# A 12-head attention and two MLPs on one core: the weights' product w3·w_out decoded by another sequence, its maxima taken from copies, its last row groups and column halves in turn

## The chip, the core and the metric

One core of a Trainium2 chip runs the whole program. The metric is device time in microseconds (us) of that core, the median of several runs. Engines: PE is TensorE, DVE is VectorE, ACT is ScalarE, POOL is GpSimd, SP issues most of the transfers.

## The reference

```python
attn = softmax(scale * einsum('bhij,hg->bgij', q @ k.T, w_pre))   # 4 batches, 12 heads, 448 positions
x = einsum('bhij,hg->bgij', attn, w_post) @ v                      # 1792 tokens x 768
h = (x @ w1) * (x @ w2)                                            # 1792 x 1024
x2 = (h @ w3) @ w_out                                              # w3 1024x1024, w_out 1024x768
g = relu(x2 @ w_in) ** 2                                           # 1792 x 2048
out = g @ w_out2                                                   # 1792 x 768, float32
```

The MLP weights arrive as 64-bit floats. The kernel works out `M = w3 @ w_out` first and then `h @ M`; this first product of two weights is the stage in question, "the weights' product".

## The kernel before

The program is emitted by one Python function, and each engine runs its own list of instructions strictly in the order in which they were emitted; semaphores order them between engines. So an instruction that waits holds up all that stands behind it on its engine.

**Stages.** Attention; then w1 and w2 (lines 1009 to 1076, giving h); then the weights' product (lines 1100 to 1129); then the scaling of M (lines 1130 to 1150); then `h @ M` (line 1009 again, called for x2); then the second MLP.

**The weights' product.** M has eight row groups of 128 rows (index f) and two column halves of 384 (index o). The loop takes row groups in pairs: p = 0 to 3, with j = 0, 1 inside the pair. For each of the 8 values of c (the contraction, 128 at a time) and each j there are six matmuls at line 1115: three products (high×high, high×low, low×high of the 32-bit weights, each split in two) times two halves o. The stationary operand is a piece of w3, the moving one a row block of w_out (`wo` for c = 0 to 3, `late` for c = 4 to 7). One pass p is 96 matmuls, the stage 384.

**Chunks.** w3 comes in 16 chunks of 128x512 numbers, each serving four values of c of one j: 24 matmuls. I number them 0 to 15 in the order in which they are decoded; pass p uses 4p to 4p+3. A chunk's steps are: a transfer of 512 KB into `raw` (two buffers, line 634); `decode` (lines 640 to 664), which turns the two 32-bit words of a 64-bit float into one 32-bit float; a cast to the high half by ACT (line 817); a subtraction for the low half by POOL (line 820). The high and low halves have room for four chunks. Before, `decode` alternates between the engines:

ACT: zt = |hi| (L648) → DVE: clamp zt (L653), shift and xor into xa (L656) → ACT: |xa| (L660) → DVE: put the sign in (L662) → ACT: cast (L817) → POOL: low half (L820). DVE's L649 (the low word's bits) needs only the raw data. The scratch tile `zt` has one buffer.

Chunks 0 to 2 are decoded in the stage before. What is emitted when is set by streams of steps that are advanced by `tick` between matmuls, against a modelled time, with a limit (`allow`) on how far ahead the weights may go; `need` forces what the next matmul uses.

**Maxima.** `keep_m` copies the four finished accumulators of a pass from PSUM to SBUF (`M32`) on ACT and takes the largest absolute value of each row on DVE (`largest`, L1027), straight from PSUM. It is emitted two values of c into the next pass, and after the last pass for that one. After it come the row maxima's product with `rows`, a transpose and a spread over all partitions on PE, a power of two, and the scaling of M to 16 bits (lines 1033 and 1037).

Of the kernel before, what the change touches and what calls it, by code (L numbers as in the profile page):

```python
# [35 lines left out]
def talking_heads_attention_moe_moe2(  # L36
# [48 lines left out]
    sm = ctx.enter_context(tc.tile_pool(name="sm", bufs=2))  # L85
# [430 lines left out]
    first = {}  # L516
# [32 lines left out]
    for b in range(B):  # L549
        f = first[4 * b]  # L550
# [9 lines left out]
    for s in range(NSUP - 1):  # L560
        for p in range(NDC):
            lo = first[s + 1] + LAG + 1
# [10 lines left out]
    last = NSUP - 1  # L573
# [24 lines left out]
    pools = {}  # L598

    chunks = []  # L600
    for fc in range(NFC):
        chunks += [("w1", fc), ("w2", fc), ("wo", fc)]
    for p in range(NFC // 2):
        for g in range(2):
            chunks += [("w3", 4 * p + 2 * j + g) for j in range(2)]
        if p == 0:
            chunks += [("wl", f) for f in range(NFC // 2, NFC)]
    for p in range(NP2):
# [4 lines left out]
    place = {c: i for i, c in enumerate(chunks)}  # L613
# [10 lines left out]
    def load_w(i):  # L624
        kind, j = chunks[i]
        dma = nc.scalar if i < 2 else nc.sync
        if kind == "wl":
            t = wo_tiles(j)[1]
            nc.sync.dma_start(t.bitcast(F32), kept[j])
        else:  # L630
            t = pools["w"].tile([P, 2 * DM], I32, tag="raw", name="raw", bufs=LOADS)
            if kind == "w3":
                t = t[:, : 8 * P]
                nc.sync.dma_start(t, moe_w3.bitcast(I32)[j // 2, j % 2])
            else:
                dma.dma_start(t, SRC[kind].bitcast(I32)[j])
        wraw[i] = t

    def decode(raw, n, total=None):
# [26 lines left out]

    ncross = [0]
    ACT, DVE, POOL, REST, GATE = range(5)
# [121 lines left out]
    def one_steps(i):  # L790
        kind, j = chunks[i]
        load_to(i + 1)
        t = wraw.pop(i)
        if kind == "wl":
            load_to(i + 2)
            hh = wo_tiles(j)[0]
            yield ACT, 0.9, lambda: nc.scalar.copy(hh, t.bitcast(F32))

            def low():
                nc.vector.tensor_tensor(t, t.bitcast(F32), hh, op=ALU.subtract)  # L800
                wsp["wo", j] = wsp[chunks[i]] = (hh, t)

            yield DVE, 1.0, low
            return
        n = 4 * P if kind == "w3" else DM
        x, ops = decode(t, n)
        yield from read_raw(i, x, ops)
        if kind == "w3":
            hh, ll = (
                pools["w"].tile([P, 4 * P], F32R, tag="w", name="w3", bufs=WB) for _ in range(2)  # L810
            )
        elif j >= NFC // 2:
            yield POOL, 0, lambda: nc.sync.dma_start(kept[j], x)
# [64 lines left out]
    allow, ahead = [1], [4.0]  # L878
    weights = Stream(weight_steps(2))

    def tick(us, act=0.0, dve=0.0):
        now[0] += us
        for e, c in ((ACT, act), (DVE, dve)):
            busy[e] = max(busy[e], now[0] - us) + c
        for st in streams + [weights]:
            r = True
            while r:
                r = st.step()
            if r is None and st in streams:
# [96 lines left out]
    def mm():  # L986
        return ps_m.tile([P, 512], F32, tag="mm", name="mm")
# [13 lines left out]
    M32 = []  # L1001
# [15 lines left out]
    def cols_of(c):  # L1017
        return slice(c * P, (c + 1) * P)
# [7 lines left out]
    def largest(out, x):  # L1026
        nc.vector.tensor_reduce(out, x, axis=AX.X, op=ALU.max, apply_absolute_value=True)  # L1027
# [17 lines left out]
    rows = sm.tile([P, 4, NFC], F32, tag="rows", name="rows", bufs=1)  # L1045
    kx = sm.tile([P, B], F32, tag="kx", name="kx", bufs=1)
    hs = []
    for fc in range(NFC):
# [4 lines left out]
        ws = [need((kind, fc)) for kind in ("w1", "w2")]  # L1053
# [21 lines left out]
        up, lo = pow2(hm[:, B : B + 1], 14, "hs")  # L1075
# [8 lines left out]
    ahead[0] = 8.0  # L1084
    limit[0] = len(chunks)

    def keep_m(p, acc):
        mx = sm.tile([P, 4], F32, tag="mx", name="mx")
        for j in range(2):
            M32.append([stage()[:, :OH] for _ in range(2)])  # L1090
            nc.scalar.copy(M32[-1][0], acc[2 * j][:, :OH])
            for o in range(2):
                largest(mx[:, 2 * j + o : 2 * j + o + 1], acc[2 * j + o][:, :OH])
            nc.scalar.copy(M32[-1][1], acc[2 * j + 1][:, :OH])
        busy[ACT] += 2.0
        busy[DVE] += 2.0
        nc.vector.tensor_reduce(
            rows[:, 1, 2 * p : 2 * p + 2], mx.rearrange("p (j o) -> p j o", j=2),
            axis=AX.X, op=ALU.max,
        )  # L1100

    for p in range(NFC // 2):
        acc = [mm() for _ in range(4)]
        for c in range(NFC):
            if p == c == 0:
                allow[0] = place["wl", NFC - 1]
            elif c % 4 == 0:
                k = 4 * p + (3 if c == 0 else 6)
                allow[0] = place["w3", k] if k < 2 * NFC else place["out", 1]
            ws = [need(("w3", 4 * p + 2 * j + c // 4)) for j in range(2)]  # L1110
            wo = need(("wo", c))
            for j in range(2):
                for n, (a, w) in enumerate(((0, 0), (0, 1), (1, 0))):
                    for o in range(2):
                        nc.tensor.matmul(
                            acc[2 * j + o][:, :OH],
                            ws[j][a][:, cols_of(c % 4)],
                            wo[w][:, o * OH : (o + 1) * OH],
                            start=(c == 0 and n == 0),
                            stop=(c == NFC - 1 and n == 2),  # L1120
                        )
                if p < NFC // 2 - 1 or c < 4:
                    tick(1.05)
            if c == 1 and p > 0:
                keep_m(p - 1, *kept_acc)
        kept_acc = [acc]
    keep_m(NFC // 2 - 1, acc)
    for st in list(streams):
        finish(st)
    nc.vector.tensor_tensor(rows[:, 2], rows[:, 0], rows[:, 1], op=ALU.mult)  # L1130
    mx = sm.tile([P, 4], F32, tag="mx", name="mx")
    nc.vector.tensor_reduce(mx[:, :1], rows[:, 2], axis=AX.X, op=ALU.max)
    pt = mm()
    nc.tensor.transpose(pt[:1, :P], mx[:, :1], ident)
    nc.vector.tensor_reduce(mx[:1, 1:2], pt[:1, :P], axis=AX.X, op=ALU.max)
# [230 lines left out]
```

## Time and profile before

| | |
|---|---|
| median of 3 runs | 1344.16 us (1341.82 to 1347.08) |
| the profiled execution's own time | 1348.12 us |
| its span in the trace | 1346.4 us |
| busy, PE / DVE / ACT / POOL | 1282.2 / 975.5 / 707.2 / 436.4 us |
| mean granted clock of PE | 0.975 of full speed |
| weights' product, first matmul to first matmul of `h @ M` | 703.53 to 795.81 us |

All times inside the run are us from the start of the span. In the rows further down, `L1115 PE MATMUL mm<-wo,w` is an instruction of line 1115 on PE that writes `mm` from `wo` and `w`; x48 says how many are merged into the row; what stands in brackets is the engine's idle time just before it and whose instruction ended that. A granted clock of 1.00 is PE's upper level of 2.4 GHz, 0.50 the lower one of 1.2 GHz.

### The profile page before, as it was taken

How to read it: one execution, taken by the hardware profiler on the slowest of the kernel's cores; microseconds unless marked ns; L12 is line 12 of the kernel's file. 1: busy time of each engine (PE TensorE's matmuls, PEld its weight loads, DVE VectorE, ACT ScalarE, POOL GpSimd, SP SyncE). 2: the span in 40 equal slices, each digit the busy share in tenths (PEclk: the TensorE clock that was granted, in tenths of full speed). 3: DMA queues.
4: the chain of work that ended last, by engine and by line, in shares of the span. 5: the costliest groups of instructions: out<-in, count | busy, mean ns of one | idle time of the engine just before them, and what ended most of it. 6: DMA issues, size and time to landing. Idle time of an engine off the chain costs nothing.

```text
span 1346.4 us, 25819 instructions
## 1 busy us (share of the span) xinstructions
PE 1282.2 (95%) x10170; PEld 790.4 (59%) x10170; DVE 975.5 (72%) x2011; ACT 707.2 (53%) x1365; POOL 436.4 (32%) x511
## 2 busy tenths in 40 slices
PE   5998999999999899999998979999999999999998
PEld 3666666666666654555557955555555555555555
DVE  5887798788688846778736546634668797797866
ACT  3876876787786534444424444425773534535430
POOL 3798789789687511000101200000000000000000
PEclk8999999999899879999999989999999999999999
DMA  6366455545545733345303313401431223213004
GB/s 175 102 169 151 117 142 141 144 126 139 137 120 153 228 73 100 75 110 147 99 26 120 106 36 81 77 3 19 98 78 36 75 59 87 75 36 84 27 13 164
DMA packets 76094, 132.92 MB, mean 99 GB/s; under 512 B 30116, under 2 KB 59940, under 8 KB 75972
## 3 DMA queue, kind: packets, MB, share of 16 engines
q1 hardware_dynamic: 69556, 121.87, 33.1%
q0 software_dynamic: 2992, 5.42, 2.6%
q10 hardware_dynamic: 3424, 3.98, 1.1%
q8 instruction: 80, 1.31, 0.5%
q14 instruction: 42, 0.34, 0.1%
HBM read 80.78 MB, written 11.92 MB: 69 GB/s over the span
## 4 chain that ended last, share of the span: by engine, by line
PE 80%; DVE 8%; DMA 5%; ACT 4%; issue 2%; POOL 1%; ACTq 0%; SPq 0%; POOLq 0%; DVEq 0%
PE mm L1009 41%; PE mm L1243 16%; PE p L269 8%; PE o L362 6%; DMA Bt<-S 4%; PE s L229 4%; PE a L471 3%; DVE ATl L384 1%; DVE xa L662 1%; DVE zt L653 1%; DVE xa L656 1%; ACT xa L660 1%; DVE EL L349 1%; DMA kraw<-in_k_dram 1%; DVE st L283 1%
## 5 line engine op out<-in xcount | busy, mean ns | idle before, releaser
L1009 PE MATMUL mm<-x,w 128*128 128x448 f16 x2304 | 441.9, 355 | 3.0 <-DVE w L738 1.8
L1009 PEld LDWEIGHTS <-w 128*128 128x128 f16 x2304 | 226.5, 98 | 216.7 <-issue 6.5
L1243 PE MATMUL mm<-w,g 128*128 128x384 f16 x1344 | 219.7, 326 | 0.0
L1243 PEld LDWEIGHTS <-g 128*128 128x128 f16 x1344 | 131.5, 98 | 87.4 <-issue 0.2
L269 PE MATMUL p<-Bt,wpre_k 120*120 120x448 f32 x360 | 165.0, 578 | 18.6 <-DMA Bt<-S 15.2
L335 POOL TENSOR_SCALAR EH<-E,st 120x448 f16<-120x448 f32 x180 | 132.7, 747 | 83.1 <-DVE st L321 60.0
L362 PEld LDWEIGHTS <-EH 120*112 120x112 f16 (+1 forms) x1440 | 127.5, 132 | 52.5 <-issue 45.6
L384 DVE TENSOR_TENSOR ATl<-o,ATh 112x480 f16<-112x480 f32 x180 | 116.2, 646 | 49.8 <-ACT ATh L378 49.6
L378 ACT CAST ATh<-o 112x480 f16<-112x480 f32 x180 | 101.1, 562 | 82.1 <-PE o L362 78.0
L362 PE MATMUL o<-wph,EH 120*112 120x120 f16 x720 | 127.5, 222 | 7.8 <-DVE ATl L384 7.8
L291 ACT ACTIVATE E<-p,st 120x448 f32<-120x448 f32 x180 | 115.9, 644 | 32.8 <-DVE st L283 19.0
L362 PE MATMUL o<-wph,EL 120*112 120x120 f16 x720 | 125.3, 219 | 0.0
L362 PE MATMUL o<-wpl,EH 120*112 120x120 f16 x720 | 125.2, 219 | 0.0
L1252 DVE SCALAR_TENSOR_TENSOR acc<-mm,sv,acc 128x384 f32<-128x384 f32 x196 | 112.3, 612 | 14.2 <-PE mm L1243 13.5
L674 POOL DMA_DIRECT2D across<-tot x23 | 12.8, 557 | 334.0 <-ACT xa L660 334.0
L283 DVE TENSOR_REDUCE st<-p 120x1 f32<-120x448 f32 x180 | 110.5, 614 | 11.4 <-PE p L269 11.0
L660 ACT ACTIVATE xa<-xa 128x768 f32<-128x768 f32 (+1 forms) x72 | 57.3, 796 | 116.2 <-DVE xa L656 106.6
L1009 PE MATMUL mm<-h,M 128*128 128x448 f16 x576 | 110.6, 356 | 1.7 <-ACT M L1037 1.7
L347 POOL TENSOR_TENSOR EL<-F,EH 120x448 f16<-120x448 f32 (+1 forms) x90 | 100.7, 1119 | 7.5
L269 PEld LDWEIGHTS p<-Bt,wpre_k 120*120 120x120 f32 x360 | 59.3, 188 | 65.9 <-issue 33.5
L240 ACT COPY S<-s 110x896 f32<-110x896 f32 (+1 forms) x92 | 83.9, 912 | 22.3 <-PE s L229 22.3
L362 PEld LDWEIGHTS <-EL 120*112 120x112 f16 x720 | 95.4, 132 | 0.0
(178 smaller groups left out, 2042.3 us busy)
## 6 DMA issues: line engine op xcount, KB each, us to landing
Bt<-S SPq DMA_DIRECT2D x176, 210.0 KB
raw<-in_moe_w_out_dram SPq DMA_DIRECT2D x24, 768.0 KB
raw<-in_moe_w_in_dram SPq DMA_DIRECT2D x16, 768.0 KB
raw<-in_moe_w_dram SPq DMA_DIRECT2D x14, 768.0 KB
raw<-in_moe_w_dram SPq DMA_DIRECT2D x16, 512.0 KB
kraw<-in_k_dram SPq DMA_DIRECT2D x12, 448.0 KB
vraw<-in_v_dram SPq DMA_DIRECT2D x8, 672.0 KB
out_dram<-acc SPq DMA_DIRECT2D x28, 192.0 KB
```

Source lines behind the costliest of these rows:

```text
L240: nc.scalar.copy(Stile[s][:R, 2 * p : 2 * p + 2, :], Ps.pop((s, p))[:R, :, :S])
L269: nc.tensor.matmul(pt[: n * H, :S], wpre_k.rearrange("p t g -> p (t g)")[: n * H, : n * H], Bt.pop(u)[: n * H], start=True, stop=True,)
L283: nc.vector.tensor_reduce(nsum[u][:n, 0, j : j + 1], Pp[u][:n, :S], axis=AX.X, op=ALU.max, negate=True)
L291: nc.scalar.activation(e[:n], Pp.pop(u)[:n, :S].rearrange("p (a b) -> p a b", a=EG), AF.Exp, bias=t[:n, 0, j : j + 1], scale=1.0, accum_ou ...
L335: nc.gpsimd.tensor_scalar(seven(EH[u][:n]), Ex[u][:n], inverse(u), 1.0, op0=ALU.mult, op1=ALU.mult)
L347: nc.gpsimd.tensor_tensor(a, f, b, op=ALU.subtract)
L362: nc.tensor.matmul(pt[:CP, c * n : (c + 1) * n], a[:n, c * CP : (c + 1) * CP], w[:n, :n], start=(i == 0), stop=(i == 2),)
L378: nc.scalar.copy(ATs[s][0][:, :, :, m * NR : m * NR + nr], src)
L384: nc.vector.tensor_tensor(ATs[s][1][:, :, :, a], src, ATs[s][0][:, :, :, a], op=ALU.subtract)
L1009: nc.tensor.matmul(pt[:, :S], w[a][:, cs], x[z][:, sl], start=(c == 0 and i == 0), stop=(c == len(parts) - 1 and i == 2),)
L1243: nc.tensor.matmul(pt[:, :OH], gs[j][a][:, ts_], ws[j][0][:, w, os_], start=(n == 0), stop=(n == 5),)
L1252: nc.vector.scalar_tensor_tensor(d, pt[:, :OH], sv[:, v : v + 1], d, op0=ALU.mult, op1=ALU.add)
```

## The change

Four things change, all around the weights' product.

1. w3's chunks are decoded by `decode_alone`: the sign is put in early, two bit operations on DVE take the place of ACT's second absolute value, and the engines change hands twice less.
2. `keep_m` copies the accumulators on ACT, and the maxima are taken from the copies, as steps of a stream of their own, emitted behind the copies.
3. In the last pass (p = 3) the row groups come one after the other (j = 0 for all c, then j = 1), and within the last row group the column halves. The chunks of that pass are decoded in that order.
4. At the end only the last half's maximum is taken after the last matmul, from PSUM; the maxima of all the others are reduced ahead of it. The streams go on being advanced in the last pass, so that the decode of `w_in`'s first pair is emitted there.

```diff
+    def decode_alone(raw, n):
...
+            (ACT, 0.9 * r, lambda: nc.scalar.activation(zt, hi.bitcast(F32), AF.Abs)),
+            (DVE, 0.55 * r, lambda: nc.vector.tensor_scalar(
+                xi, lo, 29, 0x40000000, op0=ALU.logical_shift_right, op1=ALU.bitwise_or
+            )),
+            (DVE, 0.95 * r, lambda: nc.vector.scalar_tensor_tensor(
+                xi, hi, -(2 ** 31), xi, op0=ALU.bitwise_and, op1=ALU.bitwise_or
+            )),
+            after(ACT),
+            (DVE, 0.55 * r, lambda: nc.vector.tensor_scalar(
+                zt, zt, F64_LEAST, F64_MOST, op0=ALU.max, op1=ALU.min
+            )),
+            (DVE, 0.55 * r, lambda: nc.vector.tensor_scalar(
+                zi, zi, 4, 1, op0=ALU.logical_shift_left, op1=ALU.logical_shift_right
+            )),
+            (DVE, 0.95 * r, lambda: nc.vector.tensor_tensor(xi, zi, xi, op=ALU.bitwise_xor)),
+            after(DVE),
...
-        x, ops = decode(t, n)
+        x, ops = (decode_alone if kind == "w3" else decode)(t, n)
...
+        for o in os_:
+            nc.scalar.copy(M32[f][o], acc[o][:, :OH])
...
+        def steps():
+            yield after(ACT)
+            for o in os_:
+                yield DVE, 0.45, lambda: largest(mx[:, f, o : o + 1], M32[f][o])
...
+                for os_ in ((0,), (1,)) if last else ((0, 1),):
+                    for c in range(NFC):
...
+                        ws = need(("w3", 4 * p + 2 * j + c // 4))
+                        m_tile(ws, c, acc[j], c == 0, c == NFC - 1, os_)
+                        if c % 2 == 1 or not last:
+                            tick(1.05)
...
+                        if c == 3 and last and os_ == (0,):
+                            keep_m(2 * p, acc[0], (0, 1))
+                        if c == 3 and last and os_ == (1,):
+                            keep_m(2 * p + 1, acc[1], (0,))
...
+    nc.vector.tensor_reduce(rows[:, 1], mx, axis=AX.X, op=ALU.max)
+    largest(mx[:, f, 1:2], acc[1][1][:, :OH])
+    nc.scalar.copy(M32[f][1], acc[1][1][:, :OH])
     nc.vector.tensor_tensor(rows[:, 2], rows[:, 0], rows[:, 1], op=ALU.mult)
-    mx = sm.tile([P, 4], F32, tag="mx", name="mx")
-    nc.vector.tensor_reduce(mx[:, :1], rows[:, 2], axis=AX.X, op=ALU.max)
+    nc.vector.tensor_reduce(most[:, 1:2], rows[:, 2], axis=AX.X, op=ALU.max)
+    nc.vector.scalar_tensor_tensor(
+        most[:, :1], mx[:, f, 1:2], rows[:, 0, f : f + 1], most[:, 1:2], op0=ALU.mult, op1=ALU.max
+    )
```

**First place: DVE where pass 0's maxima come into chunk 7's decode.** Before, the four maxima (L1027, from the PSUM tile `mm`) stand inside the chunk, between L649 and L653:

```order
L649 TENSOR_SCALAR xa<-raw 128x512
L1027 TENSOR_REDUCE mx<-mm 128x1 x4
L1097 TENSOR_REDUCE rows<-mx 128x2
L653 TENSOR_SCALAR zt<-zt 128x512
L656 SCALAR_TENSOR_TENSOR xa<-zt,xa 128x512
L662 SCALAR_TENSOR_TENSOR xa<-raw,xa 128x512
```

In the changed kernel the lines are L658 and L661 (raw data alone), L665 (the clamp, which waits for ACT's zt), L668 and L671; the maxima (now L1063, from the copy `st`) stand between two chunks:

```order
L658 TENSOR_SCALAR xa<-raw 128x512
L661 SCALAR_TENSOR_TENSOR xa<-raw,xa 128x512
L665 TENSOR_SCALAR zt<-zt 128x512
L668 TENSOR_SCALAR zt<-zt 128x512
L671 TENSOR_TENSOR xa<-zt,xa 128x512
L1063 TENSOR_REDUCE mx<-st 128x1 x4
```

A chunk now has five DVE instructions instead of four, two of them ahead of the wait for ACT.

**Second place: ACT at the end of the last pass.** Before, it holds chunk 15's steps, the four copies and then the scaling of M:

```order
L648 ACTIVATE zt<-raw 128x512
L660 ACTIVATE xa<-xa 128x512
L817 CAST w_11712<-xa 128x512
L1091 COPY st<-mm 128x384
L1094 COPY st<-mm 128x384
L1037 ACTIVATE M_11798<-st,rows 128x384
```

Now three chunks of `w_in` (L684, L696, 128x768) are begun there, between the copies:

```order
L853 CAST w_11727<-xa 128x512
L684 ACTIVATE zt<-raw 128x768
L1132 COPY st<-mm 128x384 x2
L696 ACTIVATE xa,tot<-xa 128x768
L684 ACTIVATE zt<-raw 128x768
L1132 COPY st<-mm 128x384
L696 ACTIVATE xa,tot<-xa 128x768
L684 ACTIVATE zt<-raw 128x768
L1196 COPY st<-mm 128x384
L1073 ACTIVATE M_11824<-st,rows 128x384
```

The last copy (L1196) and all of M's scaling now stand behind the absolute value of `w_in`'s third chunk, which needs that chunk's transfer.

**Third place: DVE at the same point, in the changed kernel.** Before, after the last matmuls, there stood four maxima, L1097, L1130 and L1132. Now:

```order
L698 SCALAR_TENSOR_TENSOR xa<-raw,xa 128x768
L685 TENSOR_SCALAR xa<-raw 128x768
L1194 TENSOR_REDUCE rows<-mx 128x8
L1063 TENSOR_REDUCE mx<-mm 128x1
L1197 TENSOR_TENSOR rows<-rows 128x8
L1198 TENSOR_REDUCE most<-rows 128x1
L1199 SCALAR_TENSOR_TENSOR most<-mx,rows,most 128x1
```

One maximum from PSUM is left behind the last matmul, with three small operations; L685 ahead of it reads the raw data of `w_in`'s third chunk.

## Rows read from the trace of the kernel before

**Rows 1.** Timeline of PE: start, us, instructions, and idle before them
```profile
703.53 8.65 PE L1115 MATMUL mm<-wo,w 128*128 128x384 f32 x48
713.75 0.62 PE L1115 MATMUL mm<-late,w 128*128 128x384 f32 x2 [1.58 <-ACT late L797]
715.18 8.39 PE L1115 MATMUL mm<-late,w 128*128 128x384 f32 x46 [0.82 <-DVE late L800]
...
725.95 0.97 PE L1115 MATMUL mm<-wo,w 128*128 128x384 f32 x4 [1.32 <-ACT w L817]
...
737.84 10.52 PE L1115 MATMUL mm<-late,w 128*128 128x384 f32 x42 [2.56 <-ACT w L817]
748.19 8.48 PE L1115 MATMUL mm<-wo,w 128*128 128x384 f32 x48
...
781.37 8.43 PE L1115 MATMUL mm<-late,w 128*128 128x384 f32 x38 [0.45 <-POOL w L820]
792.74 0.37 PE L1134 MATMUL mm<-ident,mx 128*1 128x128 f32 x1 [2.95 <-DVE mx L1132]
...
795.81 14.48 PE L1009 MATMUL mm<-h,M 128*128 128x448 f16 x68 [1.74 <-ACT M L1037]
```

**Rows 2.** Waits from 690 to 815 us: who for whom, total, times, longest
```profile
ACT st L1094 <- DVE mx L1027: 8.7, 8, 1.1
...
PE mm L1115 <- ACT w L817: 7.6, 4, 2.6
...
PE mm L1115 <- POOL w L820: 1.8, 4, 0.5
```

**Rows 3.** Waits of PE from 796 us to the end, the only row
```profile
PE mm L1009 <- ACT M L1037: 1.7, 1, 1.7
```

**Rows 4.** Chain that ended last, one chunk's period: start, us, what
```profile
741.74 0.62 ACT w L817
742.36 0.58 ACT zt L648
742.97 1.10 DVE zt L653
...
744.10 0.70 DVE xa L656
...
744.88 0.64 ACT xa L660
...
745.55 0.70 DVE xa L662
...
746.33 0.63 ACT w L817
```

**Rows 5.** Chain that ended last, at the stage's end
```profile
791.08 1.03 DVE mx L1027 x2
792.13 0.17 DVE rows L1097
```

**Rows 6.** Durations in ns (least, median, most) by line or tile
```profile
L649 DVE TENSOR_SCALAR xa<-raw x8: 418/420/422, 720.5 to 758.1; 128x512 int32<-128x512 int32 x8
...
L653 DVE TENSOR_SCALAR zt<-zt x72: 416/554/1518, 438.3 to 1271.7; 128x768 f32<-128x768 f32 x56, 128x512 f32<-128x512 f32 x16
...
L800 DVE TENSOR_TENSOR late<-late x4: 946/948/1398, 713.7 to 716.8; 128x768 fp32r<-128x768 f32 x4
...
L820 POOL TENSOR_TENSOR w<-xa,w x16: 1267/1284/1299, 667.3 to 780.0; 128x512 fp32r<-128x512 f32 x16
...
L662 DVE SCALAR_TENSOR_TENSOR xa<-raw,xa x10: 691/948/959, 762.0 to 856.9; 128x768 int32<-128x768 int32 x6, 128x512 int32<-128x512 int32 x4
```

**Rows 7.** Windows: stretch, its us, PE busy, granted clock, DMA share, GB/s
```profile
740.00:744.00 4.00, 4.00 (x14) 0.50 0.30 101
```

**Rows 8.** Issue of a 768 KB transfer of w_in, and its last traffic
```profile
771.94 0.33 SPq L636 DMA_DIRECT2D raw<-in_moe_w_in_dram  x1
...
775.50:776.00 0.50, 0.50 (x4) 1.00 0.18 57
```

More of the change, by code (lines that the diff above doesn't have):

```diff
@@ L603, in talking_heads_attention_moe_moe2 @@
     for p in range(NFC // 2):
-        for g in range(2):
-            chunks += [("w3", 4 * p + 2 * j + g) for j in range(2)]
+        order_of = ((0, 0), (1, 0), (0, 1), (1, 1)) if p < NFC // 2 - 1 else ((0, 0), (0, 1), (1, 0), (1, 1))
+        chunks += [("w3", 4 * p + 2 * j + g) for j, g in order_of]
         if p == 0:
@@ L637, in load_w, with __init__, __call__, after @@
         wraw[i] = t
+    class Behind:
+        def __init__(self, eng):
+            self.eng = eng
+        def __call__(self):
+            return max(0.0, busy[self.eng] - now[0]) + 0.3
+    def after(eng):
+        return REST, Behind(eng), None
+    def decode_alone(raw, n):
+        lo, hi = (raw.rearrange("p (f two) -> p f two", two=2)[:, :, w] for w in (0, 1))
+        x = pools["w"].tile([P, DM], F32, tag="xa", name="xa", bufs=3)[:, :n]
+        zt = pools["w"].tile([P, DM], F32, tag="zt", name="zt", bufs=1)[:, :n]
+        xi, zi = x.bitcast(I32), zt.bitcast(I32)
+        r = n / DM
+        return x, [
+            (ACT, 0.9 * r, lambda: nc.scalar.activation(zt, hi.bitcast(F32), AF.Abs)),
[14 more added lines that the diff above has]
+            after(DVE),
+        ]
     def decode(raw, n, total=None):
@@ L1085, in talking_heads_attention_moe_moe2 @@
     limit[0] = len(chunks)
-    def keep_m(p, acc):
-        mx = sm.tile([P, 4], F32, tag="mx", name="mx")
-        for j in range(2):
-            M32.append([stage()[:, :OH] for _ in range(2)])
[L1091 to L1111, printed above, removed]
-            for j in range(2):
[L1113 to L1126, printed above, removed]
@@ L1127, in talking_heads_attention_moe_moe2, with keep_m @@
-    keep_m(NFC // 2 - 1, acc)
+    NP = NFC // 2
+    mx = sm.tile([P, NFC, 2], F32, tag="mx", name="mx", bufs=1)
+    most = sm.tile([P, 4], F32, tag="most", name="most", bufs=1)
+    nc.gpsimd.memset(mx[:, NFC - 1, 1:2], 0.0)
+    def keep_m(f, acc, os_):
+        if len(M32) == f:
+            M32.append([stage()[:, :OH] for _ in range(2)])
+        for o in os_:
+            nc.scalar.copy(M32[f][o], acc[o][:, :OH])
+        busy[ACT] = max(busy[ACT], now[0]) + 0.5 * len(os_)
+        def steps():
+            yield after(ACT)
+            for o in os_:
+                yield DVE, 0.45, lambda: largest(mx[:, f, o : o + 1], M32[f][o])
+        streams.append(Stream(steps()))
@@ new lines, in m_tile @@
+    def m_tile(ws, c, acc, first, last, os_=(0, 1)):
+        wo = need(("wo", c))
+        for n, (a, w) in enumerate(((0, 0), (0, 1), (1, 0))):
+            for o in os_:
+                nc.tensor.matmul(
+                    acc[o][:, :OH],
+                    ws[a][:, cols_of(c % 4)],
+                    wo[w][:, o * OH : (o + 1) * OH],
+                    start=(first and n == 0),
+                    stop=(last and n == 2),
+                )
+    kept_acc = []
+    for p in range(NP):
+        acc = [[mm() for _ in range(2)] for _ in range(2)]
+        if p < NP - 1:
+            for c in range(NFC):
+                if p == c == 0:
+                    allow[0] = place["wl", NFC - 1]
+                elif c % 4 == 0:
+                    allow[0] = place["w3", 4 * p + (3 if c == 0 else 6)]
+                ws = [need(("w3", 4 * p + 2 * j + c // 4)) for j in range(2)]
+                for j in range(2):
+                    m_tile(ws[j], c, acc[j], c == 0, c == NFC - 1)
+                    tick(1.05)
+                if c == 1:
+                    for f, x in kept_acc:
+                        keep_m(f, x, (0, 1))
+            kept_acc = [(2 * p + j, acc[j]) for j in range(2)]
+        else:
+            for j in range(2):
+                last = j == 1
+                for os_ in ((0,), (1,)) if last else ((0, 1),):
+                    for c in range(NFC):
+                        if c % 4 == 0 and os_[0] == 0:
+                            allow[0] = (
+                                place["w3", 4 * p + 3] if not last else place["out", 1]
+                            )
+                        ws = need(("w3", 4 * p + 2 * j + c // 4))
+                        m_tile(ws, c, acc[j], c == 0, c == NFC - 1, os_)
+                        if c % 2 == 1 or not last:
+                            tick(1.05)
+                        if c == 1 and not last:
+                            for f, x in kept_acc:
+                                keep_m(f, x, (0, 1))
+                        if c == 3 and last and os_ == (0,):
+                            keep_m(2 * p, acc[0], (0, 1))
+                        if c == 3 and last and os_ == (1,):
+                            keep_m(2 * p + 1, acc[1], (0,))
@@ L1128, in talking_heads_attention_moe_moe2 @@
     for st in list(streams):
         finish(st)
+    f = NFC - 1
+    nc.vector.tensor_reduce(rows[:, 1], mx, axis=AX.X, op=ALU.max)
+    largest(mx[:, f, 1:2], acc[1][1][:, :OH])
+    nc.scalar.copy(M32[f][1], acc[1][1][:, :OH])
     nc.vector.tensor_tensor(rows[:, 2], rows[:, 0], rows[:, 1], op=ALU.mult)
-    mx = sm.tile([P, 4], F32, tag="mx", name="mx")
-    nc.vector.tensor_reduce(mx[:, :1], rows[:, 2], axis=AX.X, op=ALU.max)
+    nc.vector.tensor_reduce(most[:, 1:2], rows[:, 2], axis=AX.X, op=ALU.max)
@@ L1133, in talking_heads_attention_moe_moe2 @@
+    nc.vector.scalar_tensor_tensor(
+        most[:, :1], mx[:, f, 1:2], rows[:, 0, f : f + 1], most[:, 1:2], op0=ALU.mult, op1=ALU.max
+    )
+    mx = most
     pt = mm()
```

## The prediction

> **What bounds the kernel now.** I read PE's timeline around the stage first [rows 1]. The weights' product begins at 703.53 us and the product after it at 795.81: 92.28 us, although its 384 matmuls need much less. Where PE works without a gap at the upper clock, 48 of them take 8.48 us (0.1767 each) or 8.65 us (0.180 each); 384 are 67.8 to 69.2 us. The other 24 us are three things.
>
> First, waits for weights. PE waits 7.6 us for ACT's cast of w3 and 1.8 us for POOL's low half [rows 2], and 1.58 and 0.82 us for the `late` half of w_out [rows 1]: 11.8 us. Nearly every wait also costs a restart of 0.16 us or so (8.65 and 8.48 contain one drain each).
>
> Second, the clock. After the wait of 2.56 us that ends at 737.84, 42 matmuls take 10.52 us where 42 × 0.1767 = 7.4 would do [rows 1], and the granted clock is then 0.50, the lower level [rows 7]: 3.1 us. The last 38 take 8.43 instead of 6.7 us after the second such wait: 1.7 us.
>
> Third, the tail. The last matmul ends at 781.37 + 8.43 = 789.80 and `h @ M` begins at 795.81: 6.01 us.
>
> 67.8 + 11.8 + 4.8 + 6.0 is 90.4, and some nine restarts of 0.16 make 91.8: the 92.28 are accounted for.
>
> Then I asked who is late. The chain runs through one chunk's decode at a time [rows 4]: from cast to cast, 741.74 to 746.33, is 4.59 us, and no step of one chunk overlaps a step of the next. PE uses a chunk in 24 × 0.1767 = 4.24 us. So the decode is the pace, and the maxima worsen it once a pass: each second copy of `keep_m` waits 1.1 us for DVE, eight times, 8.7 us in all [rows 2], in the middle of a chunk. A pass of PE's is 96 × 0.1767 = 17.0 us; of the decode's, 4 × 4.59 = 18.4 plus the copies and maxima.
>
> Last I looked at what comes behind: from 796 us to the end PE waits 1.7 us, once, right at the start [rows 3]. So what the stage gives back reaches the end in full.
>
> **The change part by part.**
>
> *The decode.* Gone are L656, L660 and L662 of the chain. New behind the clamp are a shift (L668) and a two-tensor xor (L671); L658 and L661 read raw data alone and run while ACT still casts the chunk before. Prices: L668 like L649, an integer operation of the same form and size, 0.42 us [rows 6]. The trace has no xor of two tensors; the nearest rows are L662 at this size, 0.69 us, and L800, 0.948 for 768 numbers, so 0.63 for 512; its dear end is L800's slowest, 1.40 [rows 6]. I take 0.70, as the size and the integer type are L662's. L661 is L662 itself, moved.
>
> The clamp costs 1.10 us in the chain [rows 4], far above L649's 0.42: POOL's subtraction of the chunk before, 1.28 us [rows 6], starts as the cast ends, and the clamp gets through when it is over. I keep 1.10.
>
> A period is then cast 0.62, zt 0.58, clamp 1.10, shift 0.42, xor 0.70 and 0.1 of hand-over: 3.5 us. DVE's own sum, 0.42 + 0.69 + 1.10 + 0.42 + 0.70 = 3.3, fits into it. With four maxima of 0.52 [rows 5] in DVE's queue, a pass of the decode is 4 × 3.5 + 2.1 = 16.1 us against PE's 17.0. PE becomes the bound, by 0.9 us a pass.
>
> *What of the waits stays.* The decode starts the stage level with PE: three chunks are ready, the fourth is not. Chunk 3 is done 0.4 us sooner (0.70 + 0.64 + 0.70 of the old chain become 0.70 + 0.42 + 0.70 behind the clamp, less a hand-over). The casts of `late` stand behind it on ACT, so of the 2.4 us some 2.0 stay. DVE is then free at about 717.3. Chunk 4's five operations, 0.42 + 0.69 + 0.42 + 0.42 + 0.70 = 2.65, put its cast at 720.6, chunk 5's a period later at 724.1, and its low half 1.3 us later at 725.4. PE begins the second pass at 703.53 + 8.65 + 2.0 + 8.39 = 722.6, uses chunk 4 for six matmuls, and wants chunk 5 at 723.7: it waits 0.4 and then, after four matmuls, 0.6. So 1.0 us of what was 1.32 and 0.45. From chunk 6 on the decode leads. Three or four restarts: 0.5. The bounds are 0.2 us, if chunk 5 is just in time, and the old 1.8.
>
> The two waits of 2.56 us are gone, and with them the two stretches at the lower clock.
>
> *The maxima.* Copies now follow each other on ACT, and the maxima wait in DVE's queue between two chunks. They delay the next chunk's L658 and L661 by 2.1 us; that is in the pass above. If DVE had no such slack, they would cost PE up to 2.1 us a pass. The copies of pass 2 stand on ACT ahead of chunk 14's cast and wait for PE's last matmul of that pass. Only chunks 14 and 15 are behind them, and since j = 0 comes first, PE wants these one group later, 8.5 us; in the old order it would have stood.
>
> *Last groups in turn.* The number of matmuls and weight loads is the same. 24 to 48 matmuls in a row now add into one accumulator; `h @ M` adds 24 into one and has no wait at all [rows 3]. I take nothing for it.
>
> *The tail.* Before, from the last matmul to the transpose, PE stood 2.95 us [rows 1]: copies and two pairs of maxima, the second pair alone 1.03 us [rows 5], and three operations of 0.17. Now one maximum, 0.52, and three small operations of 0.17 with their gaps, 0.6, are left: 1.15. The tail becomes 6.01 − 1.8 = 4.2 us. The cover that this needs: L684 and L685 of `w_in`'s third chunk stand ahead on ACT and DVE. Its transfer waits for L698 of `w_in`'s first chunk, which has the last use of that raw buffer. From the end of j = 0 on: two copies, 1.0; L696 and L698, 0.95 each at L662's larger size [rows 6]; a transfer from issue at 771.94 to its last traffic before 776.0, 4.1 us [rows 8]; L685, 0.55. That is 7.5 us, and j = 1 ends after 48 × 0.1767 = 8.5. One microsecond to spare; each us later would lengthen the tail by one.
>
> *The sum.* 67.8 (matmuls) + 2.0 + 1.0 (waits) + 0.5 (restarts) + 4.2 (tail) = 75.5 us instead of 92.28: 16.8 us less. At 0.180 a matmul and the old waits it would be 78 us, and 74.5 at best. The profiled execution took 1348.12 us, 4.0 over the median of 1344.16, with a span of 1346.4; it would give 1331.3. Against the median I say 1344.16 − 16.8 = 1327.4, about 1327.5.
>
> A rule against this: the Trainium skill ("SBUF — State Buffer", "Who interferes with whom") says that a DVE instruction with two inputs in SBUF and a POOL instruction that reads SBUF exclude each other for a whole instruction, whichever starts first. L800's 1.40 beside its usual 0.95 us agrees [rows 6]; that POOL is the one to wait, no run here shows, as its 1.267 to 1.299 hardly vary. By that rule POOL would wait for L661 of the next chunk, the period grows by 0.4 to 3.9, the pass to 17.7, and the sum by some 3 us, to 1330.
>
> **The rivals.**
>
> *A, as summed: PE is the bound.* Own range 1324 to 1331.
>
> *B, the decode stays the pace.* L661 and L671 take two tensors and overlap POOL; if either or both wait for it, the period rises. For it: the clamp's 1.10. Against: only one POOL instruction of 1.28 us comes per chunk, and the clamp already pays for it. At 3.9 (POOL put off by 0.4 behind L661) a pass is 17.7, 0.7 over PE's, three passes about 2, and the start loses 1: 1330. At 4.6, the old period, with the maxima still out of the chunks, a pass is 20.5, 3.5 over PE's, 10 us in three passes: 1338. This holds the skill's rule.
>
> *C, the tail waits for `w_in`.* If that transfer, or the steps ahead of it, come 2 to 5 us later than I reckon, ACT and DVE stand behind it and the tail grows by 1 to 4 us: 1328.5 to 1331.5.
>
> *D, slower.* The place is DVE's shift and xor. If both are dear, each paying for POOL as the clamp does, the period is 0.62 + 0.58 + 1.10 + 1.10 + 1.40 + 0.1 = 4.9 us, a pass 21.7, three passes 14 us over PE's, and 1342 comes out. It decides at a period of about 5.2; at 5.7 a pass is 24.9, 24 us over in three, and the time 1351. Against it: POOL would have to run more than once a chunk.
>
> *E, the tail and clock change nothing:* if PE falls to the lower clock at the stage's end for longer than now, 1 to 2 us come off the gain; inside A's range.
>
> **How the numbers follow.** A and E 0.68, B 0.16 (a quarter of it above 1334), C 0.11, D 0.05. Predicted is A's 1327.5. From 1322 (matmuls below 0.1767 and no wait left) to 1335 the range leaves out D and B's dear quarter, and takes in A's other bounds. What a measurement of this kernel can tell from no change is about 0.5%, 6.7 us: faster means below 1337.4. A, C and nearly all of B lie there, 0.92; B's end and D's middle give 0.05 for the same, D's upper end 0.03 for slower.
>
> **What would show it.** Right: no wait of PE above 1.5 us between 716 us and the stage's end; casts 3.4 to 3.7 us apart where DVE has no maxima; granted clock 1.00 through the stage; POOL's subtraction ahead of PE's need from chunk 6 on; 2.9 us of idle PE before the transpose become about 1.2. Wrong: casts 4.2 us or more apart (B, D); ACT's L1196 or DVE's L1194 standing behind a transfer of `w_in` (C); waits of PE after the stage, where there were none.

## The result, and the profile after

The changed kernel takes 1326.8 us (median of 4 runs, 1326.03 to 1327.23), the kernel before 1344.84 beside it (4 runs): a ratio of 0.986, 95% interval 0.9835 to 0.9886. The profiled execution took 1326.03 us, with a span of 1324.3 and a mean granted clock of 0.989; PE is busy for 1271.6 us.

The timeline of PE in the changed kernel, from the stage's first matmul to `h @ M`:

```profile
698.03 8.71 PE L1146 MATMUL mm<-wo,w 128*128 128x384 f32 x48
708.05 0.62 PE L1146 MATMUL mm<-late,w 128*128 128x384 f32 x2 [1.31 <-ACT late L833]
709.48 8.30 PE L1146 MATMUL mm<-late,w 128*128 128x384 f32 x46 [0.81 <-DVE late L836]
717.62 1.21 PE L1146 MATMUL mm<-wo,w 128*128 128x384 f32 x6
719.09 0.96 PE L1146 MATMUL mm<-wo,w 128*128 128x384 f32 x4 [0.26 <-ACT w L853]
720.57 6.90 PE L1146 MATMUL mm<-wo,w 128*128 128x384 f32 x38 [0.51 <-POOL w L856]
727.31 8.54 PE L1146 MATMUL mm<-late,w 128*128 128x384 f32 x48
735.69 8.54 PE L1146 MATMUL mm<-wo,w 128*128 128x384 f32 x48
...
767.13 2.26 PE L1146 MATMUL mm<-late,w 128*128 128x384 f32 x12
770.56 0.27 PE L1204 MATMUL mm<-ident,most 128*1 128x128 f32 x1 [1.17 <-DVE most L1199]
...
773.42 26.92 PE L1045 MATMUL mm<-h,M 128*128 128x448 f16 x132 [1.84 <-ACT M L1073]
```

Beside [rows 1]: the stage is 698.03 to 773.42, 75.39 us instead of 92.28. Of the waits for weights four are left, all at the start; from 720.57 to the last matmul there is no idle time at all. From 727.31 on, groups of 48 start 8.38 us apart, and the idle time before the transpose is 1.17 us instead of 2.95.

The stage accounts for 16.9 us, the two medians differ by 18.0, and the two profiled spans by 22.1. The rest of that last number lies ahead of the stage: it begins 5.5 us sooner. The code there is the same but for the decode of chunks 0 to 2, and the start does not go by that: with the old decode it lies between 696.25 and 703.53 us in the executions profiled here, with the new one between 693.55 and 703.95. Behind it nothing moved: from its end to the span's end it is 550.6 us before and 550.9 after, and PE has no wait there.

Two windows (stretch, its us, busy time by engine, granted clock, DMA share, GB/s). The first is the stretch that ran at 0.50 before [rows 7]; now it runs at the upper level, and so does every stretch of 4 us from 700 to 772. Only in the tail does the clock fall:

```profile
740.00:744.00 4.00, 4.00 (x25) 4.00 (x24) 3.90 (x9) 1.69 (x4) 1.29 (x1) 1.00 0.37 128
772.00:776.00 4.00, 2.57 (x8) 0.94 (x9) 3.19 (x8) 3.25 (x7) 0.55 (x1) 0.72 0.56 190
```

One period of the new decode, by the timelines of ACT, DVE and POOL, from one cast to the next; [rows 4] is the old one:

```profile
718.42 0.62 ACT L853 CAST w<-xa 128x512 fp32r<-128x512 f32 x1 [2.49 <-DVE xa L671]
718.94 0.67 ACT L657 ACTIVATE zt<-raw 128x512 f32<-128x512 f32 x1
722.10 0.62 ACT L853 CAST w<-xa 128x512 fp32r<-128x512 f32 x1 [2.48 <-DVE xa L671]
...
718.23 0.42 DVE L658 TENSOR_SCALAR xa<-raw 128x512 int32<-128x512 int32 x1
718.68 0.69 DVE L661 SCALAR_TENSOR_TENSOR xa<-raw,xa 128x512 int32<-128x512 int32 x1
719.64 1.15 DVE L665 TENSOR_SCALAR zt<-zt 128x512 f32<-128x512 f32 x1 [0.27 <-ACT zt L657]
720.83 0.43 DVE L668 TENSOR_SCALAR zt<-zt 128x512 int32<-128x512 int32 x1
721.29 0.69 DVE L671 TENSOR_TENSOR xa<-zt,xa 128x512 int32<-128x512 int32 x1
...
719.11 1.40 POOL L856 TENSOR_TENSOR w<-xa,w 128x512 fp32r<-128x512 f32 x1 [2.28 <-ACT w L853]
```

The period is 722.10 − 718.42 = 3.68 us (4.59 before). The clamp (L665) takes 1.15 us and ends 0.28 after POOL's subtraction. Where maxima stand ahead of it, POOL is done by then; DVE around 727:

```profile
725.59 1.93 DVE L1063 TENSOR_REDUCE mx<-st 128x1 f32<-128x384 f32 x4
...
728.69 0.42 DVE L665 TENSOR_SCALAR zt<-zt 128x512 f32<-128x512 f32 x1
```

The clamp then takes 0.42. So the four maxima (1.93 us) lengthen a pass by about 1.0 only: casts four chunks apart stand at 722.10 and 737.79, 15.7 us, where the kernel before has 21.06 (737.16 to 758.22).

### The profile page after: what moved, and what is told of

It is laid out like the page before. It is cut to its first block, busy times and chain, and to the rows that moved or that the text cites. A ratio compares the mean times of both kernels' runs of the same rounds, so it can differ in the third digit from the quotient of the medians.

```text
span 1324.3 us, 25802 instructions
## 1 busy us (share of the span) xinstructions
PE 1271.6 (96%) x10170; PEld 784.6 (59%) x10170; DVE 984.5 (74%) x2025; ACT 695.7 (53%) x1349; POOL 436.0 (33%) x512
## 3 DMA queue, kind: packets, MB, share of 16 engines
q8 instruction: 80, 1.31, 0.4%
## 4 chain that ended last, share of the span: by engine, by line
PE 84%; DVE 5%; DMA 4%; issue 2%; ACT 2%; POOL 1%; SPq 0%; ACTq 0%; POOLq 0%; DVEq 0%
PE mm L1045 41%; PE mm L1313 17%; PE p L269 8%; PE o L362 6%; PE s L229 4%; DMA Bt<-S 4%; PE mm L1146 4%; PE a L471 3%; DVE ATl L384 1%; DVE EL L349 1%; DVE st L283 1%; ACT E L291 1%; DVE Vl L450 0%; PE s L471 0%; POOL EH L335 0%
## 5 line engine op out<-in xcount | busy, mean ns | idle before, releaser
L349 DVE SCALAR_TENSOR_TENSOR EL<-E,st,EH 120x448 f16<-120x448 f32 (+1 forms) x90 | 85.7, 952 | 12.5 <-POOL EH L335 11.9
```

The lines of the kernel that those rows point to most:

```text
L349: nc.vector.scalar_tensor_tensor(a, e, inverse(u), b, op0=ALU.mult, op1=ALU.subtract)
```

## The experiments

"Stage" is always the time from the first matmul of the weights' product to the first of `h @ M` in the profiled execution. It tells these kernels apart better than the total does, since the stage's start alone varies from 693.6 to 704.0 us between executions, whichever decode stands ahead of it. Each ratio is to executions of the kernel before that were taken beside that run, so it is not the quotient of the medians in this table.

| kernel | stage, us | idle before the transpose, us | median, us | ratio to before (95%) |
|---|---|---|---|---|
| before | 92.28 | 2.95 | 1344.84 | 1 |
| changed | 75.39 | 1.17 | 1326.8 | 0.986 (0.9835 to 0.9886) |
| decode_only | 79.94 | 2.95 | 1334.89 | 0.9919 (0.9896 to 0.9943) |
| maxima_only | 81.94 | 2.04 | 1333.76 | 0.9911 (0.988 to 0.9942) |
| last_only | 93.11 | 4.98 | 1346.49 | 1.0009 (0.999 to 1.0028) |
| old_decode | 85.49 | 5.94 | 1335.94 | 0.9927 (0.9898 to 0.9956) |
| old_end | 75.81 | 2.04 | 1333.42 | 0.9884 (0.9847 to 0.9921) |
| xor_quarter | 79.27 | 3.58 | 1333.96 | 0.9896 (0.9865 to 0.9926) |
| xor_twice | 81.29 | 1.17 | 1336.79 | 0.9918 (0.9887 to 0.995) |
| late_in | 82.14 | 8.01 | 1331.22 | 0.9883 (0.9845 to 0.9921) |
| no_early | 75.92 | 1.18 | 1325.83 | 0.9849 (0.9821 to 0.9876) |
| fourth_early | 70.89 | 1.17 | 1325.66 | 0.9845 (0.9818 to 0.9871) |
| best | 71.12 | 0.90 | 1326.64 | 0.9849 (0.982 to 0.9877) |
| robust | 71.90 | 0.90 | 1324.44 | 0.9838 (0.9812 to 0.9864) |

**The parts alone.** decode_only is the kernel before with `decode_alone`:

```diff
-        x, ops = decode(t, n)
+        x, ops = (decode_alone if kind == "w3" else decode)(t, n)
```

> The kernel before with only w3's decode exchanged; maxima, order of the last pass and tail as before. If the decode was the pace (my theory), casts come 3.7 us apart instead of 4.6, but the copies and maxima still stand inside a chunk and add some 2.7 us a pass, so a pass of the decode is about 17.4 us against PE's 16.8, and the old tail of 6 us stays: weights' product 78 to 81 us instead of 92.3, gain 11 to 14 us. If the maxima inside the chunks were what cost the time (rival), gain below 5 us. If the last pass and the tail were (second rival), no more than 3.

As expected: −12.3 us. Four casts are 17.43 us apart (718.74 to 736.17), still more than PE's pass, since the maxima stand in the chunks as before; the view of waits has the old row, unchanged, and PE's waits became short:

```profile
ACT st L1130 <- DVE mx L1063: 8.7, 8, 1.1
...
PE mm L1151 <- POOL w L856: 1.7, 4, 0.5
...
PE mm L1151 <- ACT w L853: 1.0, 2, 0.7
```

maxima_only is the kernel before with copies on ACT in every pass, and the maxima from them as steps:

```diff
             for o in range(2):
-                largest(mx[:, 2 * j + o : 2 * j + o + 1], acc[2 * j + o][:, :OH])
-            nc.scalar.copy(M32[-1][1], acc[2 * j + 1][:, :OH])
+                nc.scalar.copy(M32[-1][o], acc[2 * j + o][:, :OH])
...
+                    yield DVE, 0.45, lambda j=j, o=o: largest(
+                        mxs[:, 2 * p + j, o : o + 1], M32[2 * p + j][o]
+                    )
```

> The kernel before with only the maxima taken from copies, behind them, in all passes; decode, order and tail as before. My theory: the decode stays the pace at 4.6 us a chunk; a pass falls from 21.1 us to 20.0 to 20.6, gain 1 to 3 us, the waits of 2.5 us for the cast get shorter, not none. Rival (the maxima cost the time): gain 8 us or more.

A miss: −10.3 us, the figure of the rival. The timelines of DVE and POOL show why:

```profile
726.98 1.93 DVE L1037 TENSOR_REDUCE mxs<-st 128x1 f32<-128x384 f32 x4
728.82 0.61 DVE L659 TENSOR_SCALAR xa<-raw 128x512 int32<-128x512 int32 x1
729.36 0.41 DVE L663 TENSOR_SCALAR zt<-zt 128x512 f32<-128x512 f32 x1
...
727.85 1.30 POOL L830 TENSOR_TENSOR w<-xa,w 128x512 fp32r<-128x512 f32 x1 [3.25 <-ACT w L827]
```

Between two chunks the maxima fill time in which DVE would wait for ACT's zt or stand in a clamp behind POOL; the clamp after them takes 0.41. Four chunks take 18.66 us from cast to cast, instead of 21.06 and against 4 × 4.59 = 18.4 without any maxima: 2.4 us a pass, 7.2 in three, of which PE's waits for the cast and the low half show 5.8 (9.4 before, 3.6 now). The idle time before the transpose gives 0.9, and the lower clock costs some 1.6 us here instead of 4.8.

last_only is the changed kernel with the old decode and the old maxima, so only the order of the last pass and the end are new:

```diff
-        x, ops = (decode_alone if kind == "w3" else decode)(t, n)
+        x, ops = decode(t, n)
...
-        for o in os_:
-            nc.scalar.copy(M32[f][o], acc[o][:, :OH])
+        for n, o in enumerate(os_):
+            if n == 0:
+                nc.scalar.copy(M32[f][o], acc[o][:, :OH])
+                for z in os_:
+                    largest(mx[:, f, z : z + 1], acc[z][:, :OH])
```

> The changed kernel with the old decode and the maxima from PSUM between the copies as before: only the order of the last pass and the tail are changed. My theory: 1.8 us from the tail and 2 to 3 from chunk 15, which is wanted later; gain 3 to 5.5 us. Second rival (the end is what counts): 8 us or more.

A miss: +0.8 us. The end costs more than it gives here, by the other half of rival C: not the transfer of `w_in`'s third chunk, but the steps of `w_in` ahead of the last maximum come late, because chunk 15 is decoded late. The last matmul ends at 788.13; DVE and PE then:

```profile
788.81 0.95 DVE L698 SCALAR_TENSOR_TENSOR xa<-raw,xa 128x768 int32<-128x768 int32 x1
...
790.84 0.96 DVE L692 SCALAR_TENSOR_TENSOR xa<-zt,xa 128x768 int32<-128x768 int32 x1
...
791.98 0.56 DVE L1063 TENSOR_REDUCE mx<-mm 128x1 f32<-128x384 f32 x1
...
793.12 0.37 PE L1203 MATMUL mm<-ident,most 128*1 128x128 f32 x1 [4.98 <-DVE most L1198]
```

DVE has no idle time in that stretch. ACT does wait 1.01 us for the transfer, until 789.31, but DVE is busy with the second chunk until 789.76. The 2 to 3 us expected of chunk 15 did not come either: PE waits 1.87 and 0.79 us for it, against 2.56 and 0.45 before.

old_decode is the changed kernel with the first of these two edits alone, so new maxima and the new end.

> The changed kernel with the old decode alone put back. My theory: the gains of the maxima and of the end add up and no more, 4 to 8 us, with casts 4.6 us apart and PE waiting in each pass. Rivals: 12 us or more, as the decode would not matter.

The size came out (−6.8 us), for another reason: its idle time before the transpose is 5.94 us, so it is 3.5 us behind maxima_only, which has the old end. With the slow decode, the new end loses. Here too it is mostly DVE's `w_in` steps ahead of the last maximum; of the time behind the last matmul the transfer itself holds DVE for 0.51 us:

```profile
777.37 0.56 DVE L685 TENSOR_SCALAR xa<-raw 128x768 int32<-128x768 int32 x1 [0.51 <-DMA raw<-in_moe_w_in_dram]
```

old_end is the kernel before with the edits of decode_only and maxima_only together: new decode, new maxima, old last pass and end.

> New decode and new maxima, but the old order in the last pass and the old end (the last four maxima from copies, all behind the last matmuls). My theory: PE is the bound as in the changed kernel; only the tail is the old one or a little more, 6 to 6.5 us instead of 4.0. Weights' product 77 to 78.5 us, gain 14 to 15.5 us over the kernel before. If the last pass's order carries more than the tail, gain 12 or less.

Below the range: the end is worth less than I thought. The stage is 75.81 us, 0.42 more than the changed kernel's. PE's timeline has its groups gapless and 8.32 us apart, against 8.38 in the changed kernel; eight groups at equal spacing would make the difference 0.9:

```profile
728.19 8.48 PE L1155 MATMUL mm<-late,w 128*128 128x384 f32 x48
736.51 8.48 PE L1155 MATMUL mm<-wo,w 128*128 128x384 f32 x48
...
772.00 0.27 PE L1175 MATMUL mm<-ident,mx 128*1 128x128 f32 x1 [2.04 <-DVE mx L1173]
```

The 0.9 is the idle time before the transpose, 2.04 against 1.17. The order of the last pass itself is worth nothing that shows.

**How near the decode is to being the bound.** xor_quarter and xor_twice are the changed kernel with one more two-tensor operation in each chunk's chain, on 128 or on all 512 columns:

```diff
+            (DVE, 0.3 * r, lambda: nc.vector.tensor_tensor(
+                zi[:, : n // 4], zi[:, : n // 4], zi[:, : n // 4], op=ALU.bitwise_or
+            )),
             (DVE, 0.95 * r, lambda: nc.vector.tensor_tensor(xi, zi, xi, op=ALU.bitwise_xor)),
```

> The changed kernel with one more two-tensor operation on 128 of the 512 columns in each chunk's decode (it leaves zt as it is), some 0.2 us on the chain. My theory: a pass of the decode grows from 15.7 to 16.5 us, still under PE's 16.8, so only the start of the stage loses: 0.3 to 0.6 us. If the decode were still the pace, 12 chunks times 0.2: 2.4 us or more.

Half right. The period is 4.00 us and a pass 17.0, above PE's 16.6 to 16.8, and PE still has no wait behind chunk 5's: the decode's lead lasts to the end. But the stage grew by 3.9 us, where 0.3 to 0.6 were expected: 0.9 in the waits at the start, and 2.4 in the tail. Chunk 15's cast comes at 762.53, after PE has begun j = 1 (762.25); in the changed kernel it comes at 758.07, 2.8 us ahead of j = 1 (760.84). `w_in` is decoded behind it, and its third transfer waits for that. DVE ends the second chunk's L701 only at 771.90, 1.1 us after the last matmul (770.79), and then waits 0.60 us for the transfer:

```profile
770.94 0.96 DVE L701 SCALAR_TENSOR_TENSOR xa<-raw,xa 128x768 int32<-128x768 int32 x1 [0.60 <-ACT xa L699]
772.50 0.56 DVE L688 TENSOR_SCALAR xa<-raw 128x768 int32<-128x768 int32 x1 [0.60 <-DMA raw<-in_moe_w_in_dram]
```

So the transfer by itself is 0.6 of the 2.4 us; the rest is late steps of `w_in`.

> The same with the full 512 columns, 0.6 us on the chain: period 4.3, a pass of the decode 18.1 us, 1.4 over PE's. My theory: the decode becomes the pace again, weights' product 78 to 81 us, 3 to 5.5 us longer than in the changed kernel, with waits of PE for the cast in every pass. If PE has the slack that only the first chunks need, less than 1.5 us.

+5.9 us, a little more than expected, at a period of 4.4 and a pass of 18.4. The decode is the pace again, though PE does not wait for the cast in every pass: longer waits at the start are back (2.04 and 1.72 us), a stretch at the lower clock follows (granted clock 0.50 from 722 to 724), and in the later passes PE waits for POOL twice (0.54 and 0.41 us):

```profile
720.20 0.97 PE L1149 MATMUL mm<-wo,w 128*128 128x384 f32 x4 [1.72 <-ACT w L856]
721.68 8.25 PE L1149 MATMUL mm<-wo,w 128*128 128x384 f32 x38 [0.51 <-POOL w L859]
...
749.64 6.99 PE L1149 MATMUL mm<-late,w 128*128 128x384 f32 x38 [0.54 <-POOL w L859]
```

Its tail is as short as the changed kernel's, since the third chunk of `w_in` is emitted behind the last maximum here.

**Rival C by itself.** late_in is the changed kernel with the transfer of `w_in`'s third chunk made twice:

```diff
                 dma.dma_start(t, SRC[kind].bitcast(I32)[j])
+                if (kind, j) == ("in", 2):
+                    dma.dma_start(t, SRC[kind].bitcast(I32)[j])
```

> The changed kernel with the transfer of w_in's third chunk made twice into the same buffer, one after the other, so that it lands some 3.8 us later. If the tail hangs on that transfer with 0.6 us to spare (rival C of the prediction), the last maximum comes 2.5 to 3.5 us later and the whole is that much longer. If the last maximum does not wait for it, no change.

+6.75 us, twice what was expected and all of it before the transpose. The issues on SP's queue, then DVE and PE:

```profile
773.75 0.33 SPq L638 DMA_DIRECT2D raw<-in_moe_w_in_dram  x1
774.17 0.38 SPq L636 DMA_DIRECT2D raw<-in_moe_w_in_dram  x1
...
781.05 0.56 DVE L687 TENSOR_SCALAR xa<-raw 128x768 int32<-128x768 int32 x1 [7.72 <-DMA raw<-in_moe_w_in_dram]
...
782.93 0.37 PE L1206 MATMUL mm<-ident,most 128*1 128x128 f32 x1 [8.01 <-DVE most L1201]
```

The second transfer landed 7.2 us after its issue instead of some 4. The next chunk's went out 0.4 us behind it, but before 776.7 hardly any traffic shows, so what held it is not shown. That a late transfer goes straight into the tail is.

no_early takes the early steps of `w_in` out of the last pass:

```diff
-                                place["w3", 4 * p + 3] if not last else place["out", 1]
+                                place["w3", 4 * p + 3]
```

> The changed kernel without any step of w_in's chunks in the last pass: they are begun only with h @ M, as before the change. My theory: they fit beside the last row group with 0.6 us to spare, so leaving them out gives nothing at the tail (within 0.3 us), and h @ M still hides them: no change in all. If they lengthen the tail, 0.5 us or more is gained; if their early start is needed later, waits of PE appear in the second MLP.

75.92 us, and no change at the end: the idle time before the transpose is 1.18, and PE has no wait behind the stage. The 0.5 us more lie at the start and in the matmuls: 46 of them take 9.61 us there instead of 8.30, at a granted clock down to 0.50, and groups are 8.48 us apart; the waits for chunk 5 are gone in return. So the early decode of `w_in` buys nothing here, and without it there is nothing that C could hold up.

**A better version.** fourth_early lets chunk 3 be decoded in the stage before:

```diff
-            place["wo", fc + 2] if fc < NFC - 2 else place["w3", 2 if fc == NFC - 2 else 1]
+            place["wo", fc + 2] if fc < NFC - 2 else place["w3", 2 if fc == NFC - 2 else 3]
```

> The changed kernel with chunk 3 of w3 decoded in the stage before too (four chunks are ready, as many as there is room for). My theory: what PE still waits at the start is chunk 3's decode standing ahead of the casts of the late half, and the decode starting level: both waits of 2.1 us go and most of the 0.8 us after them, with their restarts; weights' product 71.5 to 73 us instead of 75.4, 2.5 to 4 us faster than the changed kernel. Rival: the late half's transfer is the limit, and at most 0.5 us is gained; or the fourth chunk delays h on DVE and ACT and PE waits before the stage.

−4.5 us in the stage, a little more than expected. All the waits at its start are gone, and from 600 us on PE does not wait ahead of the stage either; its timeline has no idle time from the first matmul to the last:

```profile
701.89 8.65 PE L1146 MATMUL mm<-wo,w 128*128 128x384 f32 x48
710.38 8.48 PE L1146 MATMUL mm<-late,w 128*128 128x384 f32 x48
```

best has that edit, and takes two of the small operations at the end ahead of the last maximum; robust is best and no_early together:

```diff
+    nc.vector.tensor_tensor(rows[:, 2], rows[:, 0], rows[:, 1], op=ALU.mult)
+    nc.vector.tensor_reduce(most[:, 1:2], rows[:, 2], axis=AX.X, op=ALU.max)
     largest(mx[:, f, 1:2], acc[1][1][:, :OH])
     nc.scalar.copy(M32[f][1], acc[1][1][:, :OH])
-    nc.vector.tensor_tensor(rows[:, 2], rows[:, 0], rows[:, 1], op=ALU.mult)
-    nc.vector.tensor_reduce(most[:, 1:2], rows[:, 2], axis=AX.X, op=ALU.max)
```

> The same with the two small operations on the other rows' maxima put ahead of the last maximum, where DVE idles 0.6 us: 0.4 us less idle PE before the transpose, so 0.3 to 0.5 us beyond the one with the fourth chunk early. It may drown in the spread of the timing; the idle time before the transpose, 1.17 us in the changed kernel, should be 0.8.

> The changed kernel with chunk 3 of w3 early, the two small operations ahead of the last maximum, and no step of w_in in the last pass, so that no transfer stands before the last maximum. My theory: nothing on the path but 384 matmuls and the tail: weights' product 70.5 to 71.5 us, of which 66.5 to 68 are matmuls, idle PE before the transpose 0.9 us, no wait of PE in h @ M beyond its first; 20 to 22 us less than the kernel before in this stage. If w_in begun late costs something after all, waits of PE appear behind the stage.

The idle time before the transpose fell to 0.90 us in both, where 0.8 and 0.9 were expected. But the stage of best is no shorter than that of fourth_early, and robust's 71.90 us lies above its range: their groups of matmuls are 8.38 and 8.48 us apart, fourth_early's 8.32. In robust, PE's waits from 600 to 1320 us are these three rows and no more:

```profile
PE mm L1045 <- ACT M L1073: 1.8, 1, 1.8
PE mm L1204 <- DVE most L1199: 0.9, 1, 0.9
PE mm L1207 <- DVE most L1205: 0.4, 1, 0.4
```

The stage of these three is 3.5 to 4.5 us shorter than the changed kernel's, but their totals (ratios 0.9838 to 0.9849) can't be told from its 0.986: the intervals overlap.

## Why the prediction was right

The likeliest case, A, is what happened: the decode got ahead of PE, and the stage is matmuls, the waits at its start and a shorter tail. Term by term, predicted and measured:

| term | predicted | measured |
|---|---|---|
| 384 matmuls | 67.8 | 8 × 8.38 = 67.0 |
| waits for `late` | 2.0 | 1.31 + 0.81 = 2.12 |
| waits for chunk 5 | 1.0 | 0.26 + 0.51 = 0.77 |
| tail | 4.2 | 4.03 |
| restarts, and what else is left over | 0.5 | 1.47 |
| stage | 75.5 | 75.39 |

- **Matmuls and restarts.** The first and the last-but-one row miss by 0.8 and 1.0, and that is one error counted twice. I had divided 8.48 us, the duration of a group, by 48; as I said myself, it contains a drain of 0.16. From start to start a group of the kernel before is 8.32 (748.19 [rows 1] to 756.51). So eight drains stood in the matmuls' term that belong to the restarts. The matmuls themselves did not become faster. Taken together, 68.3 was predicted and 68.5 measured.
- **The decode.** The unseen xor took 0.69 us (0.70 taken) and the shift 0.43 (0.42). The period is 3.68, not 3.5: the clamp takes 1.15, and the gaps between the steps are 0.22 together, not 0.1. (zt's 0.67 is no change: its instruction took 0.67 before too; the 0.58 of [rows 4] leaves out what lies beside the cast.) xor_twice shows what a longer period, the premise of B and D, would have done: at 4.4 PE waits again.
- **The maxima.** Their 2.1 us a pass was mis-sized: a pass is 15.7, so they cost 1.0, as the clamp behind them is fast. This and the period too short by 0.2 are opposite errors, so the pass came out near the 16.1 taken. The error on the maxima made me expect 1 to 3 us of maxima_only, which gave 10.3.
- **Parts don't add.** The decode alone is worth 12.3 us, the maxima alone 10.3, both 16.5 (old_end). Each alone leaves the decode the pace (passes of 17.4 and 18.7 us); with both PE is the bound, and what is saved beyond that is lead, not time.
- **The end.** Its 1.8 us off the tail was right in sum, but not as the new end's work: 0.9 of it comes with the maxima from copies (idle time 2.04 in maxima_only and old_end), 0.9 with the end.
- **Rival C** didn't happen, but its sign showed, and the margin was less than I reckoned. In the changed kernel DVE's L685, with L1194 behind it, waits for the transfer and is through 0.63 us before the last matmul ends, not 1.0: from issue at 763.58 to landing at 768.08 the transfer took 4.5 us, where I had 4.1. DVE's timeline:

```profile
768.15 0.56 DVE L685 TENSOR_SCALAR xa<-raw 128x768 int32<-128x768 int32 x1 [0.62 <-DMA raw<-in_moe_w_in_dram]
768.63 0.16 DVE L1194 TENSOR_REDUCE rows<-mx 128x8 f32<-128x16 f32 x1
769.43 0.56 DVE L1063 TENSOR_REDUCE mx<-mm 128x1 f32<-128x384 f32 x1 [0.63 <-PE mm L1146]
```

  Late by its transfer alone the tail was only in late_in; in last_only, old_decode and xor_quarter mostly by the steps of `w_in`.
- **The rule against.** I had given the Trainium skill's rule ("SBUF — State Buffer", "Who interferes with whom") a period of 3.9 and a sum of 1330. In the trace POOL's subtraction starts at 719.11, while L661 runs until 719.37, and takes 1.40 instead of the 1.28 usual before [rows 6]; where no L661 runs beside its start, it takes 1.27 to 1.30 in this trace too. So POOL is indeed held, but by 0.12 us, as little of L661 is left when POOL starts. The clamp has one input, so the rule as I gave it does not speak of it; it is held all the same, 1.15 us beside POOL and 0.42 alone.
- **The total** came 0.7 us below the forecast. That it is so near is in part chance: predicted were 16.8 us less, and the stage gave 16.9 in the profiled executions, but the medians differ by 18.0, and by the interval the difference is 15 to 22 us. Part of the 1.2 is made up for by the kernel before, whose median beside it was 0.7 higher than the one I had started from.

## What to carry to other kernels

Where two causes make the same wait, price each alone and both together against the next bound: the second one fixed gives only what is left up to it. Work put into an engine's queue may cost nothing if it stands where that engine would wait anyway; ask what the operation behind it then no longer waits for. Steps of a later stage pulled ahead of a stage's end hang that end on their transfers and on their own work in the queues, so price the margin, and whether pulling them ahead buys anything at all.

## What was not expected of the hardware

- **Spacing of matmuls.** Groups of 48 start 8.32, 8.38 or 8.48 us apart, mostly the same through one execution's stage and different between executions (old_end, changed, robust), all at a granted clock of 1.00; in xor_quarter they go from 8.32 to 8.38 within the stage. Why stays open; it is 1.3 us over the stage.
- **The clock after a wait.** In maxima_only, after a wait of 1.47 us and then one of 0.44, the granted clock was 0.53 and 0.62 in the next two windows of 2 us, and 38 matmuls took 8.44 us:

```profile
718.65 0.97 PE L1129 MATMUL mm<-wo,w 128*128 128x384 f32 x4 [1.47 <-ACT w L827]
720.07 8.44 PE L1129 MATMUL mm<-wo,w 128*128 128x384 f32 x38 [0.44 <-POOL w L830]
```

The kernel before has nearly the same pair at the same place, 1.32 [rows 1] and 0.45, and there they take 6.87 us, by PE's timeline:

```profile
727.37 6.87 PE L1115 MATMUL mm<-wo,w 128*128 128x384 f32 x38 [0.45 <-POOL w L820]
```

So the length of the waits does not decide it: old_decode has 1.31 and 0.44 at that place and pays, 8.46 us for the 38; no_early pays after the waits for `late`, 1.31 and 0.82, which cost the changed kernel nothing. Which waits of this size cost the clock stays open.

- **A slow transfer.** In late_in two of 768 KB were issued 0.4 us apart, and the first took 7.2 us to land; one alone took 4.1 [rows 8] to 4.5 us. By windows of 0.25 us, traffic sets in at 776.7, 2.9 us after the issue, where the one issued at 769.41 shows some after 1 us. Whether the second transfer or something else held it is not shown.
